# Decoding weights in steps of 1024 columns and starting the gate products a chunk earlier in a three-layer kernel on one core

## The chip, the core and the metric

The kernel runs on one core of a Trainium2 chip. TensorE (PE) does the matrix products, VectorE (DVE), ScalarE (ACT) and GpSimd (POOL) work on tiles in the on-chip memory, SyncE (SP) and GpSimd issue DMA transfers. The metric is the device time of one execution in microseconds (us); smaller is better.

## What is computed

Three layers, one after the other, for 4 x 768 = 3072 tokens. A retention layer (linear attention with a decay per head, 8 heads of 64), then two feed-forward layers:

```
state = gamma * state + k_t v_t^T ;  y_t = scale * q_t state
h = (x @ w1) * (x @ w2) @ w3 ;  x = h @ w_out
h = x @ w_in ;  g = h * sigmoid(1.702 h) ;  out = g @ w_out
```

x is 3072 x 512; w1 and w2 are 512 x 1024, w3 1024 x 1024, the first w_out 1024 x 512, w_in 512 x 2048, the last w_out 2048 x 512. q, k and v are float32. The weights are handed to the core as the 64-bit words of float64 numbers and turned into float32 there.

## The kernel before

**Precision.** Every large product is done three times in the fast float32 format: a matrix is split into a high part and a low part (the residue), and `mm3` multiplies high by high, high by low, low by high.

**Weights.** 36 tiles (`tiles`): 8 of w1 and w2 together (the gate), 4 of w_out, 8 of w3, 16 of the last layer. A tile has two halves. `fetch` loads a raw half, 128 x 512 words of 8 bytes, into one of five buffers; the first two by GpSimd's queue, the others by SP's. Three of the early ones are `held`: VectorE first writes a few zeros into the buffer, so that the load can't be issued before VectorE has come to that place. `magnitude` (ScalarE) takes the absolute value of the high words into `x`. `weight_steps` is a generator whose steps run on VectorE: clamp (line 196), shift (204), or-in of the low words (208), sign (218), all in place in x and by halves of 512 columns. Then `upper` (ScalarE, 145) casts x to the high part `wh` and `lower` (VectorE, 150) subtracts it to get the low part `wl`; both by halves. The low parts of a tile are made after the clamp of the next. That is ten steps a tile (`TILE_OPS`). Tiles of the last layer (`seven`) go through GpSimd into DRAM.

**Order.** The program is written out by hand; each engine runs its instructions in the order in which the program issues them. `work(n)` advances the decode by n steps, so a table of numbers decides where decode stands between other work.

**Attention.** 24 chunks of 128 tokens (c = 0 to 23; six per batch). In the turn of chunk c: vs (v with its decay, ScalarE and GpSimd) and the scores `s` of chunk c+1 (line 376, into one bank that all chunks share), the products `y` with the state (431), the mask of chunk c+1 (`pt`, 394, VectorE), the state's update `u` (407) and copy (419), the products `y` with pt (442), the outputs `xb` (463), the load of a later chunk of qkv (357, GpSimd's queue, 1 MB). Between these stand four places at which `fill(c, at)` adds other work (at = 0 to 3). xb goes to DRAM (`xd`, SP's queue) or, for two blocks of 512 tokens, is split into xh and xl at once.

**Gate within the attention.** From the chunk with c = 9 on, at the end of a turn, half a gate tile of the first token block is multiplied (`first_gate`, lines 259 to 261: for each of four k-blocks wh by xh, wh by xl, wl by xh) into one bank, `wide` (psg). At the start of the next turn `first_out` copies the bank to h (ScalarE, 995) or multiplies h by it (VectorE, 997). Fifteen halves fit before the last chunk ends; the sixteenth follows in a loop behind it.

**Behind the attention.** The other five blocks go through the gate (`gate_mm`, banks psm, eight tiles each) with a number of decode steps per tile, and eight products of w3 and w_out (`mix_mm`, psw) stand among them as soon as their tiles are decoded. From there on the layers are products of blocks in a seven-product scheme: `blend`, `Expand`, `contract`.

The numbers that steer the decode in the attention, four per chunk (one per place), are:

```
PACE = dict.fromkeys(range(5, 9), (0, 2, 0, 0))
PACE.update({9: (0, 2, 0, 5), 10: (0, 1, 0, 5)})
work(PACE.get(c, (0, 1, 0, 4))[at])
```

Of the kernel before, what the change touches and what calls it, by code (L numbers as in the profile page):

```python
# [7 lines left out]
F32 = mybir.dt.float32  # L8
F32R = mybir.dt.float32r
# [25 lines left out]
LEAST, MOST = 2.0, (1 + 0x680000 / 2**23) * 2.0**32  # L35
TILE_OPS = 10
PACE = dict.fromkeys(range(5, 9), (0, 2, 0, 0))
PACE.update({9: (0, 2, 0, 5), 10: (0, 1, 0, 5)})
NM = KF // 2
# [8 lines left out]
def tile_kernel(  # L48
# [49 lines left out]
    WO, W3, WI = 8, 12, 20  # L98
    raws, wx, parts = {}, {}, {}
    homes = {"wg": big}  # L100
# [33 lines left out]
    def magnitude(i):  # L134
        if i >= len(tiles):
            return
        xs = wx.setdefault(i, [])
        for raw in raws.get(i, [])[len(xs) :]:
            x = prep.tile([P, WC], F32, tag="x", bufs=6, name="x")
            high = raw[:, :, 1].bitcast(F32)  # L140
            nc.scalar.activation(x, high, AF.Abs, scale=2.0**16)  # L141
            xs.append(x)

    def upper(i, n):
        nc.scalar.copy(parts[i][0][:, n * WC : (n + 1) * WC], wx[i][n])

    def lower(i, n):
        at = slice(n * WC, (n + 1) * WC)
        hi, lo = (x[:, at] for x in parts[i])
        nc.vector.tensor_tensor(lo, wx[i][n], hi.bitcast(F32), ALU.subtract)  # L150

# [38 lines left out]
    def weight_steps():  # L190

        nonlocal used
        for i in range(len(tiles)):
            magnitude(i)
            for x in wx[i]:
                nc.vector.tensor_scalar(x, x, LEAST, MOST, ALU.max, ALU.min)
                yield i - (len(lows) > 0)
            for k, f in enumerate(lows):
                f()
                yield i - 1 + k  # L200
            lows.clear()
            for x in wx[i]:
                bits = x.bitcast(I32)
                nc.vector.tensor_scalar(bits, bits, 3, None, ALU.logical_shift_left)
                yield i
            for x, raw in zip(wx[i], raws[i]):
                bits = x.bitcast(I32)
                nc.vector.scalar_tensor_tensor(
                    bits, raw[:, :, 0], 29, bits, ALU.logical_shift_right, ALU.bitwise_or
                )  # L210
                yield i
            if i:
                magnitude(i + 1)
            if i < WI:
                parts[i] = wtile(tiles[i][1])
            for n, (x, raw) in enumerate(zip(wx[i], raws[i])):
# [3 lines left out]
                )  # L220
                if i < WI:
                    upper(i, n)
                used += 1
                fetch()
                fetch()
                if i:
                    magnitude(i + 1)
# [3 lines left out]
            if i < WI:  # L231
                lows[:] = [lambda i=i, n=n: lower(i, n) for n in range(2)]
            if i == 0:
                for k, f in enumerate(lows):
                    f()
                    yield k
                lows.clear()

# [3 lines left out]
    ALL = 10**6  # L242
    limit = TILE_OPS * KF + 6

# [42 lines left out]
    def gate_half(t, m, key, ps):  # L287

        w = [x.rearrange("p (m k f) -> p m k f", m=2, k=KD) for x in weight(t)]
        xh, xl = xhl[key]  # L290
        for d in range(KD):
            mm3(ps, w[0][:, m, d], w[1][:, m, d], xh[:, d], xl[:, d], d == 0, d == KD - 1)

# [566 lines left out]
    def opening(t):  # L860
# [11 lines left out]
        if t == 6:  # L872
            hi2["k3"] = prep.tile([P, TB], F32R, tag="x", bufs=6, name="h3")
            split_h(0, 3, 4, hi2["k3"].rearrange("p (a t) -> p a t", a=1))
# [81 lines left out]
    with tc.manual_schedule():  # L956
# [4 lines left out]
        with (  # L961
# [11 lines left out]
            for c in range(2, 6):  # L973
                attention.load(c)
            for _ in range(2):
                fetch(queue=nc.gpsimd)
            attention.factors(1)
# [23 lines left out]
            def fill(c, at):  # L1001
                for _ in range((c, at) in ((6, 0), (7, 0), (8, 0))):
                    fetch(held=True)
                if at == 3 and c > 2 * CPB and halves // 2 < min(complete, KF):
                    first_gate(wide)
                if at == 0:
                    while late:
                        first_out(*late.pop())
                if at == 1 and c in (*range(2, 6), *range(10, 14)):
                    hi, lo, x = first_x.pop(0)  # L1010
                    nc.scalar.copy(hi, x)
                    engine = nc.vector if c > 2 * CPB else nc.gpsimd
                    engine.tensor_tensor(lo, x, hi.bitcast(F32), ALU.subtract)
                if c > CPB:
                    work(PACE.get(c, (0, 1, 0, 4))[at])
                if (c, at) == (8, 2):
                    magnitude(1)

            attention.run(fill)
            free = [wide] + [  # L1020
                y[:, j].rearrange("p n t -> p (n t)") for y in attention.y for j in range(2)
# [8 lines left out]
        with (  # L1030
# [69 lines left out]
            for n, i in list(enumerate(ORDER))[1:]:  # L1100
                nxt = ORDER[n + 1] if n + 1 < NB else None
                for t in range(KF):
# [10 lines left out]
                    if nxt is not None and t in range(KD - 1, KF - 1):  # L1113
                        split_x(nxt, t - KD + 1)
                    work(((8, 6, 3, 3)[n - 1] + (n < 4) * (t % 2)) if n < 5 else (t < 4) + (t < 5))
                    (gate_second if n > 2 else gate_first)(t, i, ab)
                    while rows < KF and (complete > W3 + rows or (n, t) == (2, KF - 1)):
                        ps = mix_mm(rows)
                        work(7)
                        mix_out(rows, ps)  # L1120
# [156 lines left out]
```

## Time and profile before

| | us |
|---|---|
| median of 3 runs | 972.88 (972.52 to 973.39) |
| the profiled execution | 973.11 |
| its span, first to last instruction | 971.3 |
| TensorE busy | 952.3 (98%) |
| weight loads of TensorE, beside its products | 826.0 |
| VectorE busy | 719.3 |
| ScalarE busy | 424.4 |
| GpSimd busy | 229.4 |
| granted TensorE clock, mean | 0.999 |

Busy times are sums over the span, and stages differ. Where a wait is shown, the name behind the arrow is what came last before the instruction could start; "issue" means that nothing shown held it. An "x2" behind a row of the timeline is two instructions, and the time before it is that of both.

### The profile page before, as it was taken

To read this page: it belongs to the slowest core of one execution; us is meant where nothing else is said; L and a number is where in the kernel's file an instruction comes from. 1 tells how busy PE (TensorE), PEld (TensorE's weight loads), DVE (VectorE), ACT (ScalarE), POOL (GpSimd) and SP (SyncE) were. 2 spreads that over 40 slices of the span, in tenths; PEclk is the share of its full clock that TensorE was granted. 3 is DMA by queue.
4 is the path that set the end of the run, shared out by engine and by line. 5 is a ranking of instruction groups with operands and counts; after the bars stand their busy time and mean duration, and the time that the engine had idled before them with its cause. 6 is when DMAs were issued, how large, how long until landed. Compare 5 with 4: busy or idle time off the path is not lost.

```text
span 971.3 us, 15570 instructions
## 1 busy us (share of the span) xinstructions
PE 952.3 (98%) x5992; PEld 826.0 (85%) x5992; DVE 719.3 (74%) x943; ACT 424.4 (44%) x691; POOL 229.4 (24%) x281
## 2 busy tenths in 40 slices
PE   6899999999999999999999999999999999999998
PEld 5678778888888888888889999999998888888886
DVE  6898878889889886766687976948686665566662
ACT  4555444433222222654536654554555544353430
POOL 6422100478787875330020000000000000000000
PEclk9999999999999999999999999999999999999999
DMA  9999766579898999899778546464696968767871
GB/s 349 400 350 350 281 214 202 199 246 359 314 365 288 357 338 395 306 334 312 248 254 305 226 171 246 203 250 184 253 348 252 339 222 271 254 196 230 290 233 50
DMA packets 112618, 266.74 MB, mean 275 GB/s; under 512 B 7872, under 2 KB 67264, under 8 KB 103456
## 3 DMA queue, kind: packets, MB, share of 16 engines
q1 hardware_dynamic: 96560, 186.64, 54.8%
q0 software_dynamic: 15840, 78.91, 21.4%
q8 instruction: 47, 0.77, 0.3%
q14 instruction: 27, 0.22, 0.1%
q10 hardware_dynamic: 144, 0.20, 0.1%
HBM read 164.53 MB, written 101.19 MB: 274 GB/s over the span
## 4 chain that ended last, share of the span: by engine, by line
PE 90%; DVE 4%; DMA 3%; issue 1%; ACT 1%; POOL 0%; DVEq 0%; POOLq 0%; ACTq 0%; SPq 0%
PE m L259 12%; PE m L260 12%; PE m L261 12%; PE psm L261 7%; PE psm L260 7%; PE psm L259 7%; PE a L260 4%; PE a L261 4%; PE a L259 4%; PE e L260 2%; PE e L259 2%; PE e L261 2%; PE psg L259 2%; PE y L442 2%; PE s L376 1%; DMA raw<-in_w_dram 1%
## 5 line engine op out<-in xcount | busy, mean ns | idle before, releaser
L260 PE MATMUL psm<-xl,wh 128*128 128x512 f32 x320 | 124.5, 389 | 0.0
L259 PE MATMUL psm<-xh,wh 128*128 128x512 f32 x320 | 124.5, 389 | 0.0
L261 PE MATMUL psm<-xh,wl 128*128 128x512 f32 x320 | 124.5, 389 | 0.0
L261 PE MATMUL m<-h,op 128*128 128x512 f32 x320 | 124.5, 389 | 0.0
L259 PE MATMUL m<-h,op 128*128 128x512 f32 x320 | 124.5, 389 | 0.0
L260 PE MATMUL m<-l,op 128*128 128x512 f32 x304 | 118.3, 389 | 0.0
L726 ACT CAST h<-l 128x2048 fp32r<-128x2048 f32 x38 | 72.3, 1914 | 85.1 <-PE m L261 56.9
L727 DVE TENSOR_TENSOR l<-l,h 128x2048 fp32r<-128x2048 f32 x38 | 85.7, 2286 | 22.5 <-ACT h L726 22.5
L732 POOL DMA_DIRECT2D op<-sw x6 | 3.2, 532 | 393.0 <-PE a L261 212.7
L260 PE MATMUL a<-yl,op 128*128 128x384 f32 x256 | 85.6, 335 | 0.1
L259 PE MATMUL a<-yh,op 128*128 128x384 f32 x256 | 85.5, 334 | 0.0
L261 PE MATMUL a<-yh,op 128*128 128x384 f32 x256 | 85.5, 334 | 0.0
L141 ACT ACTIVATE x<-raw 128x512 f32<-128x512 f32 x72 | 46.9, 675 | 70.3 <-DMA raw<-in_wo_dram 35.7
L261 PEld LDWEIGHTS m<-h,op 128*128 128x128 f32 x320 | 60.1, 188 | 12.6
L260 PEld LDWEIGHTS psm<-xl,wh 128*128 128x128 f32 x320 | 60.1, 188 | 12.6
L259 PEld LDWEIGHTS psm<-xh,wh 128*128 128x128 f32 x320 | 60.1, 188 | 12.5
L259 PEld LDWEIGHTS m<-h,op 128*128 128x128 f32 x320 | 60.1, 188 | 12.4
L261 PEld LDWEIGHTS psm<-xh,wl 128*128 128x128 f32 x320 | 60.1, 188 | 12.3
L260 PEld LDWEIGHTS m<-l,op 128*128 128x128 f32 x304 | 57.1, 188 | 11.8
L259 PE MATMUL m<-h,wh 128*128 128x512 f32 x168 | 65.4, 389 | 0.0
L261 PE MATMUL m<-h,wl 128*128 128x512 f32 x168 | 65.4, 389 | 0.0
L175 DVE TENSOR_TENSOR l<-l,h 128x2048 fp32r<-128x2048 f32 x19 | 43.6, 2292 | 26.1 <-ACT h L274 24.6
(172 smaller groups left out, 2198.1 us busy)
## 6 DMA issues: line engine op xcount, KB each, us to landing
gd<-g SPq DMA_DIRECT2D x32, 1344.0 KB, 5.0
qkv<-in_qkv_dram POOLq DMA_DIRECT2D x20, 1024.0 KB, 9.2
l<-gd SPq DMA_DIRECT2D x26, 768.0 KB, 7.4
l<-hd SPq DMA_DIRECT2D x19, 1024.0 KB, 7.4
raw<-in_w_dram SPq DMA_DIRECT2D x30, 512.0 KB, 5.9
hd<-g POOLq DMA_DIRECT2D x12, 1280.0 KB, 7.2
raw<-in_wo_dram SPq DMA_DIRECT2D x24, 512.0 KB, 6.8
l<-gd SPq DMA_DIRECT2D x24, 512.0 KB, 5.2
```

The costliest lines, as they stand in the source:

```text
L141: nc.scalar.activation(x, high, AF.Abs, scale=2.0**16)
L175: nc.vector.tensor_tensor(lo, x, hi.bitcast(F32), ALU.subtract)
L259: nc.tensor.matmul(ps, wh, xh, start=start, stop=False, skip_group_check=True)
L260: nc.tensor.matmul(ps, wh, xl, start=False, stop=False, skip_group_check=True)
L261: nc.tensor.matmul(ps, wl, xh, start=False, stop=stop, skip_group_check=True)
L376: nc.tensor.matmul(self.s[u * D : (u + 1) * D, j, p, t], qkt[c][r, 1, p, u * D : (u + 1) * D], qkt[c][r, 0, p, t], start=True, stop=True, ...
L442: nc.tensor.matmul(out_y, vs[c][:, 2 * p + j, :], pt[c][:, j, p, :], start=(c % NCK == 0 and p < 2), stop=True, skip_group_check=True,)
L726: nc.scalar.copy(hi, x.bitcast(F32))
L727: nc.vector.tensor_tensor(x, x.bitcast(F32), hi.bitcast(F32), ALU.subtract)
L732: queue.dma_start(t.bitcast(F32), sw[PART[name]])
```

## The change

**Decode.** The two halves of x are one tile of 1024 columns (`whole`). Clamp, shift, high part and low part are one instruction each; or-in and sign, which read raw words, stay in halves. A tile has seven steps. The numbers of `work` are new accordingly.

**ScalarE's part.** `upper` and the magnitudes of the next tile are put into a list (`later`) while the attention runs, and the list is emptied at place 0 of a chunk's turn behind `first_out` (the gate's copy), or just before `lower` needs it.

**Start.** The decode starts at c = 4 instead of 5, the held loads stand at c = 5, 6, 7 instead of 6, 7, 8, the magnitudes of tile 1 at c = 7 instead of 8, gate halves at c = 8 instead of 9. The first two raw halves are loaded ahead of qkv chunks 4 and 5 on GpSimd's queue instead of behind 5.

**Within a gate half** the eight products with wh come first, then the four with wl.

```
-TILE_OPS = 10
-PACE = dict.fromkeys(range(5, 9), (0, 2, 0, 0))
-PACE.update({9: (0, 2, 0, 5), 10: (0, 1, 0, 5)})
+TILE_OPS = 7
+PACE = {4: (0, 1, 0, 0), 5: (0, 1, 0, 1), 6: (0, 1, 0, 1), 7: (0, 1, 0, 1)}
...
-            x = prep.tile([P, WC], F32, tag="x", bufs=6, name="x")
+            if not xs:
+                whole[i] = prep.tile([P, 2 * WC], F32, tag="x", bufs=3, name="x")
+            x = whole[i][:, len(xs) * WC : (len(xs) + 1) * WC]
...
-    def upper(i, n):
-        nc.scalar.copy(parts[i][0][:, n * WC : (n + 1) * WC], wx[i][n])
+    def upper(i):
+        nc.scalar.copy(parts[i][0], whole[i])
...
+    def lower(i):
+        hi, lo = parts[i]
+        nc.vector.tensor_tensor(lo, whole[i], hi.bitcast(F32), ALU.subtract)
+
+    def flush():
+        while later:
+            later.pop(0)()
+
+    def when_free(f):
+        later.append(f)
+        if not deferred:
+            flush()
...
-            for x in wx[i]:
-                nc.vector.tensor_scalar(x, x, LEAST, MOST, ALU.max, ALU.min)
-                yield i - (len(lows) > 0)
-            for k, f in enumerate(lows):
-                f()
-                yield i - 1 + k
-            lows.clear()
-            for x in wx[i]:
-                bits = x.bitcast(I32)
-                nc.vector.tensor_scalar(bits, bits, 3, None, ALU.logical_shift_left)
+            x = whole[i]
+            bits = x.bitcast(I32)
+            nc.vector.tensor_scalar(x, x, LEAST, MOST, ALU.max, ALU.min)
+            yield i - (len(lows) > 0)
+            if lows:
+                flush()
+                lows.pop()()
                 yield i
+            nc.vector.tensor_scalar(bits, bits, 3, None, ALU.logical_shift_left)
+            if i:
+                when_free(lambda i=i: magnitude(i + 1))
+            yield i
...
-                if i < WI:
-                    upper(i, n)
+                if i < WI and n:
+                    when_free(lambda i=i: upper(i))
...
-        for d in range(KD):
-            mm3(ps, w[0][:, m, d], w[1][:, m, d], xh[:, d], xl[:, d], d == 0, d == KD - 1)
+        h, l = (x[:, m] for x in w)
+        todo = [(h[:, d], x[:, d]) for d in range(KD) for x in (xh, xl)]
+        todo += [(l[:, d], xh[:, d]) for d in range(KD)]
...
-            for _ in range(2):
-                fetch(queue=nc.gpsimd)
+                if c in (3, 4):
+                    fetch(queue=nc.gpsimd)
...
-                for _ in range((c, at) in ((6, 0), (7, 0), (8, 0))):
+                for _ in range((c, at) in ((5, 0), (6, 0), (7, 0))):
                     fetch(held=True)
-                if at == 3 and c > 2 * CPB and halves // 2 < min(complete, KF):
+                if at == 3 and c >= 2 * CPB and halves // 2 < min(complete, KF):
                     first_gate(wide)
                 if at == 0:
                     while late:
                         first_out(*late.pop())
+                    flush()
...
-                if c > CPB:
-                    work(PACE.get(c, (0, 1, 0, 4))[at])
-                if (c, at) == (8, 2):
+                if c >= CPB:
+                    work(PACE.get(c, (0, 1, 0, 2 + c % 2))[at])
+                if (c, at) == (7, 2):
                     magnitude(1)
...
+            deferred = False
+            flush()
...
-                    work(((8, 6, 3, 3)[n - 1] + (n < 4) * (t % 2)) if n < 5 else (t < 4) + (t < 5))
+                    work((6, 4 + t % 2, 2 + t % 2, 2 + (t % 3 == 1), (t < 4) + (t < 5))[n - 1])
...
-                        work(7)
+                        work(5)
```

Three places show what moved. In the order of ScalarE, around the high part of tile 0 (state is the copy of the attention's state, x the magnitudes, wh the high part, vs the values of a chunk), before:

```order
L419 COPY state_130<-u 128x256
L368 ACTIVATE vs<-qkv,dv 128x64 x4
L145 CAST wh<-x 128x512 x2
L419 COPY state_131<-u 128x256
L141 ACTIVATE x<-raw 128x512 x2
```

and after:

```order
L432 COPY state_130<-u 128x256
L143 ACTIVATE x<-raw 128x512 x2
L147 CAST wh<-x 128x1024
L381 ACTIVATE vs<-qkv,dv 128x64 x4
L432 COPY state_131<-u 128x256
```

The cast of tile 0 stood ahead of the magnitudes of tile 1 (the third and fourth raw half) and now stands behind them; it has moved one chunk forward.

On VectorE, the same stretch (L394 and L407 are the masks of the scores, L463 and L476 the outputs), before, from the mask of chunk 6 to one step past that of chunk 8:

```order
L394 TENSOR_TENSOR pt<-s,mask 128x1024
L196 TENSOR_SCALAR x<-x 128x512 x2
L463 TENSOR_TENSOR xb<-y_135,dy 128x512
L130 MEMSET raw 128x2
L394 TENSOR_TENSOR pt<-s,mask 128x1024
L204 TENSOR_SCALAR x<-x 128x512 x2
L463 TENSOR_TENSOR xb<-y_134,dy 128x512
L130 MEMSET raw 128x2
L394 TENSOR_TENSOR pt<-s,mask 128x1024
L208 SCALAR_TENSOR_TENSOR x<-raw,x 128x512 x2
```

and after, over the same masks:

```order
L407 TENSOR_TENSOR pt<-s,mask 128x1024
L213 TENSOR_SCALAR x<-x 128x1024
L476 TENSOR_TENSOR xb<-y_135,dy 128x512
L219 SCALAR_TENSOR_TENSOR x<-raw,x 128x512
L130 MEMSET raw 128x2
L407 TENSOR_TENSOR pt<-s,mask 128x1024
L219 SCALAR_TENSOR_TENSOR x<-raw,x 128x512
L476 TENSOR_TENSOR xb<-y_134,dy 128x512
L227 SCALAR_TENSOR_TENSOR x<-raw,x 128x512
L407 TENSOR_TENSOR pt<-s,mask 128x1024
L227 SCALAR_TENSOR_TENSOR x<-raw,x 128x512
```

Shift, or-in and sign of tile 0 now stand where clamp, shift and the first or-in stood.

On SP's queue, from its first store of outputs on (raw is a raw half, xd a store of outputs), before:

```order
L470 DMA xd_72<-xb 128x512 x2
L131 DMA raw<-in_w_dram 128x1024
L470 DMA xd_72<-xb 128x512
L131 DMA raw<-in_w_dram 128x1024
L470 DMA xd_72<-xb 128x512
L131 DMA raw<-in_w_dram 128x1024 x6
```

and after:

```order
L483 DMA xd_72<-xb 128x512
L131 DMA raw<-in_w_dram 128x1024
L483 DMA xd_72<-xb 128x512
L131 DMA raw<-in_w_dram 128x1024
L483 DMA xd_72<-xb 128x512
L131 DMA raw<-in_w_dram 128x1024 x3
L483 DMA xd_72<-xb 128x512
L131 DMA raw<-in_w_dram 128x1024 x4
```

Each of the first raw halves on this queue has one store less ahead of it; two were loaded by GpSimd, so these are the third, the fourth and so on.

## Rows read from the trace of the kernel before

**Rows 1.** The page, part 1: busy us (share of the span) and instructions.
```profile
PE 952.3 (98%) x5992; PEld 826.0 (85%) x5992; DVE 719.3 (74%) x943; ACT 424.4 (44%) x691; POOL 229.4 (24%) x281
```

**Rows 2.** Stretches: length, busy us of the engines, granted clock, DMA share, GB/s.
```profile
0.00:10.00 10.00, 1.94 (x42) 1.80 (x46) 2.47 (x3) 2.55 (x6) 6.00 (x16) 1.00 0.78 254
10.00:60.00 50.00, 44.49 (x967) 37.14 (x962) 42.32 (x59) 27.48 (x81) 23.39 (x31) 1.00 1.01 401
120.00:180.00 60.00, 59.13 (x284) 47.96 (x283) 48.93 (x91) 25.29 (x44) 5.86 (x7) 1.00 0.60 201
180.00:960.00 780.00, 779.89 (x3756) 685.43 (x3755) 570.13 (x704) 337.77 (x481) 182.93 (x210) 1.00 0.77 273
960.00:971.30 11.30, 6.84 (x31) 5.33 (x29) 1.45 (x3) 0.00 (x0) 0.00 (x0) 0.96 0.14 47
```

**Rows 3.** Waits of TensorE, whole span: us in total, times, longest.
```profile
PE s L376 <- DMA qkv<-in_qkv_dram: 6.0, 4, 4.6
...
PE s L376 <- issue: 1.8, 2, 1.1
...
PE psg L259 <- ACT h L995: 0.7, 1, 0.7
...
PE psw L261 <- DVE wl L150: 0.2, 1, 0.2
```

**Rows 4.** Timeline of TensorE: start, us, line, out<-in, count [idle before].
```profile
36.09 0.39 PE L407 MATMUL u<-vs,qkv 128*64 128x64 f32 x6 [1.47 <-issue]
...
39.07 1.05 PE L442 MATMUL y<-pt,vs 128*64 128x128 f32 x16
...
40.60 0.79 PE L376 MATMUL s<-qkv 64*64 64x128 f32 x25 [0.49 <-DMA qkv<-in_qkv_dram]
...
42.54 0.34 PE L376 MATMUL s<-qkv 64*64 64x64 f32 x4 [1.14 <-issue]
...
44.84 0.50 PE L259 MATMUL psg<-xh,wh 128*128 128x512 f32 x1
...
47.79 0.90 PE L376 MATMUL s<-qkv 64*64 64x128 f32 x32
...
56.13 0.47 PE L259 MATMUL psg<-xh,wh 128*128 128x512 f32 x1 [0.27 <-DVE h L997]
...
125.78 0.50 PE L259 MATMUL psg<-xh,wh 128*128 128x512 f32 x1 [0.68 <-ACT h L995]
```

**Rows 5.** Timeline of ScalarE around the casts of the first gate tiles.
```profile
40.10 1.22 ACT L145 CAST wh<-x 128x512 fp32r<-128x512 f32 x2 [1.51 <-DVE x L218]
...
44.10 0.70 ACT L141 ACTIVATE x<-raw 128x512 f32<-128x512 f32 x1 [1.95 <-DMA raw<-in_w_dram]
...
53.46 0.68 ACT L141 ACTIVATE x<-raw 128x512 f32<-128x512 f32 x1 [1.82 <-DMA raw<-in_w_dram]
```

**Rows 6.** Timeline of SP's queue: a store and the fourth raw half.
```profile
27.56 4.36 SPq L470 DMA_DIRECT2D xd<-xb  x2
...
34.38 0.66 SPq L131 DMA_DIRECT2D raw<-in_w_dram  x1
```

**Rows 7.** DMA issues at 31.97 and 34.38: count, KB, us to landing.
```profile
raw<-in_w_dram SPq DMA_DIRECT2D x1, 512.0 KB, 6.5
...
raw<-in_w_dram SPq DMA_DIRECT2D x1, 512.0 KB, 9.7
```

**Rows 8.** DMA queues, 27.5 to 30.0 and 40.2 to 54: packets, MB, share.
```profile
q0 software_dynamic: 140, 1.01, 98.0%
...
q0 software_dynamic: 479, 3.53, 62.6%
q1 hardware_dynamic: 654, 2.08, 37.4%
```

**Rows 9.** VectorE from 10 to 120 us, by form: count | busy, mean ns | idle before.
```profile
L394 DVE TENSOR_TENSOR pt<-s,mask 128x1024 f32<-128x1024 f32 x23 | 28.1, 1221 | 10.1 <-PE s L376 10.1
L150 DVE TENSOR_TENSOR wl<-x,wh 128x512 fp32r<-128x512 f32 x15 | 10.1, 681 | 0.1
```

More of the change, by code (lines that the diff above doesn't have):

```diff
@@ L98, in tile_kernel @@
     WO, W3, WI = 8, 12, 20
-    raws, wx, parts = {}, {}, {}
+    raws, wx, whole, parts = {}, {}, {}, {}
+    later, deferred = [], True
     homes = {"wg": big}
@@ L142, in magnitude @@
             xs.append(x)
-    def upper(i, n):
-        nc.scalar.copy(parts[i][0][:, n * WC : (n + 1) * WC], wx[i][n])
[L147 to L150, printed above, removed]
+    def upper(i):
[10 more added lines that the diff above has]
+            flush()
     def store_parts(i, a1, a2, st):
@@ L211, in weight_steps @@
                 yield i
-            if i:
-                magnitude(i + 1)
             if i < WI:
@@ L225, in weight_steps @@
                 fetch()
-                if i:
+                if i and not deferred:
                     magnitude(i + 1)
@@ L231, in weight_steps @@
             if i < WI:
-                lows[:] = [lambda i=i, n=n: lower(i, n) for n in range(2)]
+                lows.append(lambda i=i: lower(i))
             if i == 0:
[L234 to L237, printed above, removed]
+                flush()
+                lows.pop()()
+                yield 1
     steps = weight_steps()
@@ L242, in tile_kernel @@
     ALL = 10**6
-    limit = TILE_OPS * KF + 6
+    limit = TILE_OPS * KF + 4
     def work(n):
@@ L290, in gate_half @@
         xh, xl = xhl[key]
-        for d in range(KD):
-            mm3(ps, w[0][:, m, d], w[1][:, m, d], xh[:, d], xl[:, d], d == 0, d == KD - 1)
+        h, l = (x[:, m] for x in w)
+        todo = [(h[:, d], x[:, d]) for d in range(KD) for x in (xh, xl)]
+        todo += [(l[:, d], xh[:, d]) for d in range(KD)]
+        for n, (a, x) in enumerate(todo):
+            nc.tensor.matmul(
+                ps, a, x, start=n == 0, stop=n == 3 * KD - 1, skip_group_check=True
+            )
     def gate_mm(t, key, tile):
@@ L872, in opening @@
         if t == 6:
-            hi2["k3"] = prep.tile([P, TB], F32R, tag="x", bufs=6, name="h3")
+            hi2["k3"] = prep.tile([P, 2 * WC], F32R, tag="x", bufs=3, name="h3")[:, :TB]
             split_h(0, 3, 4, hi2["k3"].rearrange("p (a t) -> p a t", a=1))
@@ L1013, in fill @@
                     engine.tensor_tensor(lo, x, hi.bitcast(F32), ALU.subtract)
-                if c > CPB:
-                    work(PACE.get(c, (0, 1, 0, 4))[at])
-                if (c, at) == (8, 2):
+                if c >= CPB:
+                    work(PACE.get(c, (0, 1, 0, 2 + c % 2))[at])
+                if (c, at) == (7, 2):
                     magnitude(1)
             attention.run(fill)
+            deferred = False
+            flush()
             free = [wide] + [
```

## Prediction

> **What bounds the kernel now.** I read the page's first part, then a table of stretches, then who TensorE waited for, then the timeline of the stretch in which it waits. TensorE is busy 952.3 us of a span of 971.3 [rows 1]. The reader is to see where the other 19.0 us lie [rows 2]: 8.06 in the first 10 us, before inputs and mask have arrived, and 4.46 behind the last products; no line of the diff touches those two. The attention stretch from 10 to 60 us loses 5.51, the stretch from 120 to 180 loses 0.87. These 6.4 us are the most that the change can win (0.65%), unless it makes TensorE's work itself shorter. It does not: the products are the same in number and shape, and only the order within a gate half differs.
>
> In the waits [rows 3] the attention stretch splits into waits for qkv (the 4.6 belongs to the first 10 us, so 1.4 are left) and gaps marked "issue" (1.8 before scores alone, and 1.47 in the update at 36.09 [rows 4]), in which no semaphore held TensorE. All of these lie ahead of the first gate half. The timeline shows the last of them: 1.47 at 36.09, 0.49 before the scores at 40.60, 1.14 in the middle of those scores. From the first gate half at 44.84 on, TensorE runs nearly without a gap; 0.27 at 56.13 and 0.68 at 125.78 remain. VectorE is busy 42.32 of those 50 us and the DMA engines have 1.01 [rows 2], so data and decode are both tight just there.
>
> **The change part by part.**
>
> *The gate one chunk earlier.* A gate half moves from the tenth chunk to the ninth, ahead of the scores at 40.60, and all sixteen halves lie within the chunks. Chunk 8's last products start at 39.07 and take 1.05, so TensorE comes free at 40.12. Where the half can start at once, it covers the 0.49 (qkv arrives meanwhile) and most likely the 1.14 (TensorE goes through 12 products in the 2.9 us instead of some 80); everything behind is a chunk ahead, so the 0.27 goes; and the sixteenth half no longer waits for the copy of its neighbour out of one bank, since two attention product groups stand between (0.68 goes). Sum: 2.58. Every microsecond by which the first half starts after 40.15 takes one back; at 42.73 nothing is left.
>
> *What the first half waits for.* It needs wh of tile 0. Before, ScalarE casts it at 40.10, in two halves of some 0.61, right behind VectorE's sign step, and only then takes the magnitudes of tile 1 [rows 5]. After, the order on ScalarE is the other way round: two magnitudes of tile 1, then one cast of 1024. So wh of tile 0 now stands behind the landing of the fourth raw half. In the trace its magnitude ran at 44.10, after a wait of 1.95 for that DMA [rows 5], which had been issued at 34.38 and took 9.7 [rows 6, 7]. After, it is issued behind only two stores instead of three, one decode step earlier, which I put at 32.6. Its latency is not shown for that place. The nearest rows are 9.7 for the same half and 6.5 for the one before it [rows 7]: it lands between 39.1 and 42.3, and at worst at 44.1 as before, if the earlier place in the queue is worth nothing. Behind it come a magnitude (0.68) and the cast (two halves are 1.22, one should be about 1.15), so the first gate half starts at 41.0, 44.2 or 46.0. I take a landing at 41.3, somewhat nearer to the later row because the same transfers stand around it, and thus a start at 43.1: 43.1 - 40.15 - 2.58 = 0.4 us **lost**. The bounds are 1.7 won and 3.3 lost.
>
> What decides inside this is how SP's queue fares against POOL's. The rows say: badly. From 27.5 to 30.0 POOL's queue has 98.0% of the engines' time [rows 8], though SP issued a store at 27.56 [rows 6]; between 40.2 and 54 SP's queue gets 37.4%, 2.08 MB in 13.8 us [rows 8]. The Trainium skill (DMA: Bandwidth & Descriptors, Queues, rings and completion order) says that each engine goes round robin between the queues for which it has work, a packet at a time. By that rule the raw half would not stand behind POOL's backlog; the result is the second rival below. The first row does not agree with it, the second does roughly.
>
> *VectorE's merged steps.* Per tile two clamps, two shifts and two subtractions become three steps of 1024. A 1024-column tensor step takes 1.221 (from PSUM), two of 512 take 2 x 0.681 = 1.36 [rows 9]; so 0.14 for a subtraction, and I put 0.1 for each of the others: 0.3 to 0.4 per tile, 12 us over 36 tiles. It lies beside TensorE's work; TensorE waits for VectorE only for 0.27 and 0.2 us behind the first ten [rows 3, 4]. On the path: 0. Against it stands that clamp and shift of tile 0 now lie a chunk earlier, ahead of masks that TensorE needs; about 1 us of delay at the mask of chunk 7, which I count at nothing because the first gate half waits for wh anyway (its price is 1.0 if wh is early).
>
> The rule that speaks against the merge is in the Trainium skill (Trace Analysis, Optimizing Scalar/DVE Operations): grouping helps an engine that is saturated, and where an engine merely makes others wait, shorter instructions get work done sooner. The trace bears it out here: of the cast at 40.10 the gate's first half needs only the first 512 columns, so with the split form it could start about 0.55 earlier than I forecast.
>
> *Low weights last; the gate's copy first.* The twelve products of a half take 2.95, from 44.84 to the scores at 47.79 [rows 4]; eight of them, some 1.9, now run before wl is needed, and before, the third product needed it. That pays for wl being one step of 1024 (1.2). Worth 0 either way. The gate's copy ahead of the magnitudes keeps the bank free in time: part of the 0.27 and 0.68 above.
>
> *Paces behind the attention.* Tiles have 7 steps for 10 and the numbers are scaled along; the products of the mixed weights come three, three and two instead of two, three and three at the same places. There wl is late by 0.2 [rows 3]; as one step of 1024 it may be 0.5 later, on one or two rows: 0 to 1 us, and I take 0.1. From 180 to 960 TensorE has no gap worth naming, and VectorE's part gets smaller.
>
> **Sum.** The profiled execution took 973.11. 973.11 + 0.4 + 0.1 = 973.6; the median of the three runs is 972.88, which is 0.23 lower: **973.4**. A measurement of this kernel can tell about 0.2% from no change, 1.95 us: this is no change.
>
> **The rivals.**
>
> *The raw data come in time* (0.22). If SP's transfers get their turn at once, the fourth half lands by 39.1, wh is there at 41.0, and the decode delay of 1.0 is then the only loss: 1.6 won, at best 2.58. 970.3 to 971.3, say 971.2. For it: the raw half before it took 6.5 only. Against it: SP's share in rows 8. (The Trainium skill's rule above is this case.)
>
> *The sixth raw half holds the third gate half* (0.17; the slower side). Before, ScalarE waited for that half until 53.46 [rows 5] and the third gate half began at 56.13, 2.67 later. After, the third half is wanted a chunk earlier: 11.4 us behind the first, at 54.5 in my forecast. Ahead of it stand again a magnitude, a clamp (now ahead of the multiplication that frees the bank), the multiplication, and a low part behind a mask: some 3.3 us. It decides from a landing at 51.2 on; if the half comes no earlier than before, the third gate half begins at 56.7 and 2.2 us are added to my forecast: 975.6. For it: with five raw halves asked for earlier, SP's queue at 0.15 MB/us has the same backlog. Against it: one store less stands ahead.
>
> *Other gaps close too* (0.06). The "issue" gaps of 1.47 and the two smaller ones lie in chunks whose timing shifts. If VectorE's later masks cover them, up to 2.6 more are won: 968.7 to 970.
>
> *The change does nothing that shows* is inside my forecast, since the merged steps are hidden.
>
> **How the numbers follow.** Forecast 0.55, with starts of the first half between 42 and 44, so 972.3 to 974.3. The range leaves out the best of the early cases and the worst of the late: 971.1 to 975.7. Faster than 970.93: 0.06 and a third of the first rival, 0.14. Slower than 974.83: 0.17 and 0.05 from late starts in my own case, 0.22. The rest, 0.64, is no change.
>
> **What would show it.** Right: in the timeline of the new kernel the first gate half stands ahead of the scores of chunk 10, begins around 43 with the wait put down to ScalarE's cast, the cast directly behind a magnitude that waited for a raw DMA; the scores behind it have no gap; the 0.68 is gone; the idle time from 10 to 60 us is 5 to 6 us. Early raws: a start at 41 or before, and 4 us idle. Late raws: a wait of over 1 us at the third gate half. Wrong altogether: idle time behind 180 us, or TensorE busy for another time than 952 us.

## The result and the profile after

The change makes the kernel slower: 982.94 us (median of 6 runs, 980.26 to 984.43) against 972.88, a ratio of 1.0100, 95% interval 1.0085 to 1.0115. The profiled execution took 983.11 with a span of 981.3, 10.0 us more than before. One of the ten executions of mag_late_cast_first, an experiment below, took 1531.21 us at a granted clock of 0.58; it is counted in that run's median (976.55; 976.45 without it) and in no ratio.

The first part of the page of the changed kernel (busy us, share of the span, instructions), to set beside [rows 1]:

```profile
PE 955.5 (97%) x5992; PEld 827.5 (84%) x5992; DVE 708.4 (72%) x850; ACT 421.9 (43%) x671; POOL 231.1 (24%) x281
```

VectorE has 719.3 - 708.4 = 10.9 us less to do, as intended. TensorE has 3.2 us more with the same 5992 products, so some of them ran slower. The table of stretches of the changed kernel (columns as in [rows 2], with the granted clock ahead of the last two):

```profile
10.00:60.00 50.00, 42.91 (x900) 35.55 (x901) 37.89 (x47) 25.07 (x74) 22.96 (x29) 0.97 0.97 381
...
120.00:180.00 60.00, 54.96 (x323) 44.25 (x322) 44.76 (x65) 22.77 (x34) 0.00 (x0) 0.94 0.57 190
180.00:240.00 60.00, 60.00 (x266) 49.67 (x266) 49.03 (x59) 21.90 (x34) 36.13 (x43) 1.00 0.75 248
240.00:960.00 720.00, 719.86 (x3491) 635.60 (x3490) 518.37 (x605) 318.12 (x447) 152.48 (x175) 1.00 0.77 276
```

Against [rows 2], the attention stretch lost 1.6 us of busy time, the stretch from 120 to 180 us lost 4.2, and in both the granted clock fell below 1. Behind 180 us nothing is lost. The longest waits of TensorE for work of other engines in the changed kernel, 10 to 240 us (us in total, times, longest), to set beside [rows 3]:

```profile
PE psw L269 <- DVE wl L151: 2.8, 1, 2.8
PE psg L303 <- ACT wh L147: 2.5, 1, 2.5
PE psw L267 <- ACT wh L147: 2.2, 1, 2.2
```

Three waits that were not there before, all for decoded weights. One (psg) is the first gate half, which the prediction spoke of. The other two (psw) are in the first product of mixed weights behind the attention.

**The attention** ends 2.8 us later: the first product of the gate behind it (psm) begins at 131.40 instead of 128.63. TensorE in the changed kernel around the first gate half (start, us, what, idle before):

```profile
39.80 1.05 PE L455 MATMUL y<-pt,vs 128*64 128x128 f32 x16
43.38 0.50 PE L303 MATMUL psg<-xh,wh 128*128 128x512 f32 x1 [2.54 <-ACT wh L147]
...
45.05 0.63 PE L303 MATMUL psg<-xh,wh 128*128 128x512 f32 x1
45.47 0.63 PE L303 MATMUL psg<-xl,wh 128*128 128x512 f32 x1
45.90 1.91 PE L303 MATMUL psg<-xh,wl 128*128 128x512 f32 x4
47.74 1.02 PE L389 MATMUL s<-qkv 64*64 64x128 f32 x32
```

and ScalarE at the same time:

```profile
41.73 0.66 ACT L143 ACTIVATE x<-raw 128x512 f32<-128x512 f32 x1 [3.52 <-DMA raw<-in_w_dram]
42.30 1.03 ACT L147 CAST wh<-x 128x1024 fp32r<-128x1024 f32 x1
43.23 1.06 ACT L381 ACTIVATE vs<-qkv,dv 128x64 f32<-128x64 f32 x4
```

The cast to wh stands behind a magnitude that waited 3.52 us for its raw half, and the gate half starts when the cast is done. That is the mechanism of the prediction, which had the start at 43.1. What it did not have is the second half of the rows: from 44.6 on a product follows its neighbour in 0.42 us instead of 0.23. The gate half takes 47.74 - 43.38 = 4.36 us instead of 2.95. The attention's account: 0.73 lost ahead of it (the products y start at 39.80 instead of 39.07), 2.54 idle, 1.41 at the lower clock, 0.67 of waiting for a wl at 69.63, less the 2.58 of closed gaps, which are indeed gone: 2.77.

**Behind the attention** 7.2 us are lost (from the first psm to the end of the span: 849.9 against 842.67). TensorE there:

```profile
166.44 0.50 PE L267 MATMUL psw<-wh 128*128 128x512 f32 x1 [2.23 <-ACT wh L147]
...
169.98 0.79 PE L269 MATMUL psw<-wh,wl 128*128 128x512 f32 x1 [2.81 <-DVE wl L151]
170.57 0.63 PE L267 MATMUL psw<-wh 128*128 128x512 f32 x1
```

5.04 us idle, and then nine products in 3.82 us (170.57 to 174.39) that take 2.05 at full clock: 1.8 more. All of it lies at the mixed products: from the first psm to the gate product behind the last psw it is 94.68 us against 87.58 before, 7.1 more, and from there on nothing. Why is the tile late? The wl of tiles 8 and 12 began at 131.38 and 159.97 before, at 134.76 and 168.71 after: the decode lost 5.4 us within four tiles, 2.9 of them in the first. There ScalarE and VectorE do this (the changed kernel):

```profile
134.63 0.67 ACT L143 ACTIVATE x<-raw 128x512 f32<-128x512 f32 x1
140.51 0.66 ACT L143 ACTIVATE x<-raw 128x512 f32<-128x512 f32 x1 [5.21 <-DMA raw<-in_wo_dram]
141.07 0.57 ACT L314 COPY h<-psm 128x512 f32<-128x512 f32 x1
```

```profile
136.62 0.69 DVE L219 SCALAR_TENSOR_TENSOR x<-raw,x 128x512 int32<-128x512 int32 x1
141.68 0.69 DVE L315 TENSOR_TENSOR h<-h,psm 128x512 f32<-128x512 f32 x1 [4.36 <-ACT h L314]
142.28 0.68 DVE L219 SCALAR_TENSOR_TENSOR x<-raw,x 128x512 int32<-128x512 int32 x1
```

and these were ScalarE and VectorE before the change at the same place:

```profile
131.55 0.59 ACT L301 COPY h<-psm 128x512 f32<-128x512 f32 x1
132.04 0.68 ACT L141 ACTIVATE x<-raw 128x512 f32<-128x512 f32 x1
137.77 0.66 ACT L141 ACTIVATE x<-raw 128x512 f32<-128x512 f32 x1 [5.06 <-DMA raw<-in_wo_dram]
```

```profile
134.33 0.69 DVE L302 TENSOR_TENSOR h<-h,psm 128x512 f32<-128x512 f32 x1 [0.99 <-issue]
```

The wait for the raw half is the same, some 5 us. Before, the gate's copy stood ahead of it; after, behind it. VectorE's multiplication by the copy waits 4.36 us instead of 0.99, and the rest of tile 9 (or-in, sign) is queued behind the multiplication. In the code, `when_free` holds back only while the attention runs; behind it, the magnitudes of the next tile are issued at once, right behind the shift, where before they came behind the or-in steps and so behind the copy.

### The profile page after: what moved, and what is told of

Its sections match the earlier page's. It is cut to its first block, busy times and chain, and to the rows that moved or that the text cites. A ratio compares the mean times of both kernels' runs of the same rounds, so it can differ in the third digit from the quotient of the medians.

```text
span 981.3 us, 15406 instructions
## 1 busy us (share of the span) xinstructions
PE 955.5 (97%) x5992; PEld 827.5 (84%) x5992; DVE 708.4 (72%) x850; ACT 421.9 (43%) x671; POOL 231.1 (24%) x281
## 4 chain that ended last, share of the span: by engine, by line
PE 87%; DVE 5%; DMA 4%; issue 2%; ACT 1%; POOL 0%; DVEq 0%; ACTq 0%; SPq 0%; POOLq 0%
PE psm L303 19%; PE m L268 12%; PE m L267 12%; PE m L269 12%; PE psg L303 4%; PE a L268 4%; PE a L269 4%; PE a L267 4%; PE e L268 2%; PE e L267 2%; PE e L269 2%; PE psw L269 2%; PE psw L267 2%; PE psw L268 2%; DMA ck<-in_qkv_dram 1%
## 5 line engine op out<-in xcount | busy, mean ns | idle before, releaser
L303 PE MATMUL psm<-xh,wl 128*128 128x512 f32 x320 | 85.5, 389 | 0.0
L267 PEld LDWEIGHTS m<-h,op 128*128 128x128 f32 x320 | 60.1, 188 | 12.5
L303 PEld LDWEIGHTS psm<-xl,wh 128*128 128x128 f32 x320 | 60.1, 188 | 12.5
L303 PEld LDWEIGHTS psm<-xh,wl 128*128 128x128 f32 x320 | 60.1, 188 | 12.5
```

Source lines behind the costliest of these rows:

```text
L267: nc.tensor.matmul(ps, wh, xh, start=start, stop=False, skip_group_check=True)
L303: nc.tensor.matmul(ps, a, x, start=n == 0, stop=n == 3 * KD - 1, skip_group_check=True)
```

## The experiments

Theory 1: the loss is the order on ScalarE, at two places. Theory 2: the steps of 1024 columns make each tile late. Theory 3: only the place of the mixed products (three, three, two) is wrong. The numbers in the table are medians, and the ratio to the kernel before, run beside them (medians of 973.5 to 973.9 in all four groups). The ratio with its interval goes by all runs of both, so that it can differ from that of the medians by up to 0.001; differences of under 1 us between two versions are not told from none by either.

| run | us | ratio | 95% |
|---|---|---|---|
| mag_late | 977.53 | 1.0043 | 1.0025 to 1.0060 |
| cast_first | 980.95 | 1.0077 | 1.0059 to 1.0095 |
| mag_late_cast_first | 976.55 | 1.0035 | 1.0025 to 1.0046 |
| rows_later | 990.89 | 1.0168 | 1.0144 to 1.0192 |
| split_behind | 981.93 | 1.0077 | 1.0057 to 1.0097 |
| fix_split_behind | 975.68 | 1.0017 | 1.0008 to 1.0027 |
| fix_split_all | 974.09 | 1.0000 | 0.9990 to 1.0011 |
| fix_gate_nine | 979.32 | 1.0059 | 1.0037 to 1.0080 |
| before_mag_early | 981.66 | 1.0087 | 1.0072 to 1.0102 |
| before_lows_last | 974.10 | 1.0003 | 0.9993 to 1.0014 |
| fix_all_rows_later | 974.74 | 1.0007 | 0.9999 to 1.0016 |
| fix_all_state_first | 973.81 | 1.0007 | 0.9994 to 1.0019 |

### The magnitudes behind the copy again (mag_late)

```
-            if i:
+            if i and deferred:
                 when_free(lambda i=i: magnitude(i + 1))
...
+            if i and not deferred:
+                magnitude(i + 1)
             if i < WI:
                 parts[i] = wtile(tiles[i][1])
```

> Behind the attention alone, the magnitudes of the next tile go back to where they stood before, behind the or-in steps, and so behind the gate's copy on ScalarE; all else as in the changed kernel (982.9 us). There the copy of the gate stood behind a magnitude that waited 5.21 us for its raw half, and VectorE's multiplication by it waited 4.36 us. Theory 1 (queue order): the decode of tile 9 gains about 3 us and all later tiles with it; the 5.04 us that TensorE waits at the first product of mixed weights fall to about 2, the time to 977.5 to 980. Theory 2 (the steps of 1024 columns are what makes a tile late, 0.5 us of waiting in each): no gain, 982 to 983. Theory 3 (the product simply stands one gate tile too early): no gain either, 982 to 983.

977.53: 5.4 us of the 10 come back from one swap, by the medians. ScalarE, then TensorE, of the profiled execution (978.97):

```profile
134.10 0.58 ACT L316 COPY h<-psm 128x512 f32<-128x512 f32 x1
...
140.80 0.66 ACT L143 ACTIVATE x<-raw 128x512 f32<-128x512 f32 x1 [5.55 <-DMA raw<-in_wo_dram]
```

```profile
165.79 0.50 PE L271 MATMUL psw<-wh,wl 128*128 128x512 f32 x1 [1.67 <-DVE wl L151]
```

The raw half is no earlier (5.55 us of waiting), but the gate's copy no longer stands behind it. The 5.04 us at the mixed products fall to 2.7 in four smaller waits, the longest 1.67, and the clock there stays at 1.00. From the first psm to the gate product behind the last psw it is 90.97 us: of the 7.1 us that the changed kernel lost there, the order made 3.7, and 3.4 are left with the order right. Theory 1 holds for the larger half; theories 2 and 3 expected nothing from this swap, but what is left is open to them.

### The cast ahead of the magnitudes (cast_first) and both (mag_late_cast_first)

```
                 if (c, at) == (7, 2):
+                    flush()
                     magnitude(1)
```

> In the attention alone: the cast to wh of tile 0 is put ahead of the magnitudes of tile 1 on ScalarE, and so no longer behind the wait for the fourth raw half (3.52 us). Theory 1 (the wait and the clock that falls behind it are the attention's loss): the first gate half starts at about 41 us instead of 43.4, the 2.54 us wait is under 0.5, the granted clock of 45 to 48 us is back from 0.50 to near 1, TensorE reaches the first product of mixed weights 2.5 to 3 us earlier, and the time is about 980. Rival (what stands behind it is late anyway, since the decode behind the attention is bound by its transfers): the wait at that product grows by as much, 982 to 983.

980.95, 2.0 us less; the intervals overlap a little, but the trace shows where it comes from. The first gate half starts without a wait, the granted clock from 44 to 48 us is 1.00 instead of 0.58, and the first psm begins at 129.01, 2.4 us earlier. Gate halves still wait for wl:

```profile
55.71 1.20 PE L303 MATMUL psg<-xh,wl 128*128 128x512 f32 x4 [1.12 <-DVE wl L151]
67.21 1.19 PE L303 MATMUL psg<-xh,wl 128*128 128x512 f32 x4 [0.67 <-DVE wl L151]
```

> Both edits, of the attention and of the magnitudes behind it. If the two losses are separate, the gains add: 974.5 to 977.5. If the decode behind the attention is late by itself, the gain of the attention reappears as a wait at the first products of mixed weights: 978 to 980.

976.55: inside the range for separate losses, and 6.4 of the 10 us are back (the two gains add up to 7.4). The attention ends level with before (psm at 128.82 against 128.63); 1.9 us of waits for wl are left at the mixed products.

### Whole tiles or halves (split_behind, fix_split_behind, fix_split_all)

```
-    def upper(i):
-        nc.scalar.copy(parts[i][0], whole[i])
+    def upper(i, n):
+        at = slice(n * WC, (n + 1) * WC)
+        nc.scalar.copy(parts[i][0][:, at], whole[i][:, at])
...
-        nc.vector.tensor_tensor(lo, whole[i], hi.bitcast(F32), ALU.subtract)
+        for at in (slice(0, WC), slice(WC, 2 * WC)):
+            nc.vector.tensor_tensor(
+                lo[:, at], whole[i][:, at], hi[:, at].bitcast(F32), ALU.subtract
+            )
...
-                if i < WI and n:
-                    when_free(lambda i=i: upper(i))
+                if i < WI:
+                    when_free(lambda i=i, n=n: upper(i, n))
```

This is fix_split_all, on top of both edits. In the other two the halves are used only behind the attention; split_behind has them alone, fix_split_behind with both edits.

> The changed kernel, with wh and wl made by halves of 512 columns again behind the attention alone; the magnitudes stay ahead of the gate's copy there, and the attention is as it was changed (982.9 us). Theory 1 (queue order is the larger part): the 5.21 us wait of the magnitude of tile 9 and VectorE's 4.36 us behind it stay; the halves win back the 0.5 us that wl waits for the whole cast in most tiles and let the first products of mixed weights start on half a tile, 1.5 to 3 us in all: 980 to 981.5. Theory 2 (steps of a whole tile are the larger part): 977 to 979.

981.93, 1.0 us less than the changed kernel, whose own runs spread over 4: no more than a hint, and not theory 2's 4 to 6 us. One of the two waits at the mixed products shrinks to 0.40, the other stays at 2.89.

> Both edits that won time (the cast of tile 0 ahead of the magnitudes in the attention, the magnitudes behind the gate's copy after it: 976.55 us), and wh and wl by halves behind the attention. There the products of mixed weights still waited 1.9 us for wl in three places, 1.0 the longest. If whole-tile steps are what is left: 974 to 975. If not, 976 to 977.

975.68: 0.9 us less, between the two expectations, and too little for the intervals to tell by itself. The wait at the first mixed product is gone; one of 0.89 on a later one is the longest left.

> As the one before, and wh and wl by halves in the attention too. There two gate halves waited 1.49 and 0.67 us for a wl of 1024 columns (1.2 us), of which the first of them needs the first 512 columns alone. If those waits are the merged steps' price: 1 to 2 us less than by halves behind the attention alone, 972.5 to 973.5, level with the kernel before. If they are the price of the earlier start: no less, 974 to 975.

974.09, level with the kernel before. The waits of this version, 5 to 240 us, those for weights:

```profile
PE psw L275 <- DVE wl L153: 1.4, 2, 0.8
...
PE psg L309 <- DVE wl L153: 0.6, 1, 0.6
```

Another 1.6 us came back, as the first expectation has it: with the order right, whole-tile casts and subtractions cost 2.5 us in all (976.55 to 974.09; these intervals are apart). How that splits between the attention and what is behind it, the traces don't show: in them the part from the first psm on shrinks by 1.5 us over the two steps (845.58, 844.67, 844.12), while the first psm stays at 128.8 to 129.2. In the attention the waits for wl did fall from 2.16 to 0.59, but TensorE waited 1.01 us for the copy of the state instead of 0.40.

### What the earlier start is worth (fix_gate_nine)

```
-                if at == 3 and c >= 2 * CPB and halves // 2 < min(complete, KF):
+                if at == 3 and c > 2 * CPB and halves // 2 < min(complete, KF):
```

> Both edits that won time (976.55 us), but gate halves from the chunk with c = 9 on, as before the change: what the earlier start is worth. By the prediction's bounds the start half a chunk earlier is worth 0 to 2.6 us. With the attention of both kernels ending level (the products behind it began at 128.8 us with both edits, at 128.6 before the change), I expect about nothing: 976 to 977.5. If the start is worth what the closed gaps say, 978 to 979.

979.32, 2.8 us more than with both edits alone. I expected nothing, and was wrong. TensorE of this run:

```profile
41.62 0.79 PE L391 MATMUL s<-qkv 64*64 64x128 f32 x25 [1.05 <-DMA qkv<-in_qkv_dram]
...
50.19 0.67 PE L446 MATMUL y<-qkv,state 64*64 64x128 f32 x16 [1.20 <-ACT state L434]
...
58.42 0.50 PE L305 MATMUL psg<-xh,wh 128*128 128x512 f32 x1 [0.83 <-DVE h L1012]
...
128.10 0.50 PE L305 MATMUL psg<-xh,wh 128*128 128x512 f32 x1 [0.67 <-ACT h L1010]
```

The gaps that the earlier start had closed are back: 1.05 and 0.32 at the scores, 0.83 and 0.67 at the bank, 2.87 together, where the prediction had 2.58. That the total moved by nearly the same is in part luck: the wait for the copy of the state grew from 0.40 to 1.20 (on ScalarE it stands behind a magnitude again), the products ahead of the gate half came 0.58 later, and against that the two waits for wl in the attention (1.49 and 0.67) went away. So the level attention of mag_late_cast_first was a gain of 2.6 to 2.9 and a loss about as large: 2.16 of waiting for wl and 0.40 for the state.

### The order alone, put into the kernel before (before_mag_early)

```
-            for x in wx[i]:
+            for n, x in enumerate(wx[i]):
                 bits = x.bitcast(I32)
                 nc.vector.tensor_scalar(bits, bits, 3, None, ALU.logical_shift_left)
+                if behind and n:
+                    magnitude(i + 1)
                 yield i
...
             attention.run(fill)
+            behind = True
```

> The kernel before, with one thing of the change done alone, and behind the attention alone: the magnitudes of the next tile are issued right behind the last shift and so ahead of the gate's copy on ScalarE. Steps, halves, paces and the places of the products are those of before. Theory 1 (queue order): the copy at 131.55 us comes behind the magnitude that ended its wait for a raw half at 137.8, VectorE's multiplication at 134.3 moves to about 139, the decode of tile 9 by 3 to 4 us, and the products of mixed weights, which waited 0.2 us for wl, wait about 3; with the lower clock that stood behind such waits in the changed kernel 976 to 979. Rival (it does harm only with whole-tile steps or the other places of the products): 973 to 974.5.

981.66: of all that the change does, this one order, in otherwise untouched code with halves, ten steps and the old places, costs 8.2 us by the medians, more than I expected. ScalarE, and TensorE, of this run:

```profile
137.43 0.66 ACT L141 ACTIVATE x<-raw 128x512 f32<-128x512 f32 x1 [5.76 <-DMA raw<-in_wo_dram]
137.99 0.57 ACT L304 COPY h<-psm 128x512 f32<-128x512 f32 x1
...
296.40 0.66 ACT L141 ACTIVATE x<-raw 128x512 f32<-128x512 f32 x1 [9.01 <-DMA raw<-in_wo_dram]
296.96 0.57 ACT L304 COPY g<-psm 128x512 f32<-128x512 f32 x1
```

```profile
163.93 0.79 PE L264 MATMUL psw<-wh,wl 128*128 128x512 f32 x1 [2.40 <-DVE wl L150]
297.59 0.50 PE L262 MATMUL psm<-xh,wh 128*128 128x512 f32 x1 [1.69 <-ACT g L304]
```

The expected wait is there (2.40, with a clock of 0.59 from 164 to 168 us): from the first psm to the gate product behind the last psw it is 91.30 us instead of 87.58. These 3.7 us are what mag_late won at the same place. The other 4.0 us lie further on, where the changed kernel loses nothing: the same order does it again at 297 us, where a magnitude waited 9 us with a copy behind it (waits of 1.69, 0.83 and 0.52 us follow, the last two for xl). So the order alone accounts for 3.7 of the 7.1 us behind the attention, shown from both sides; that 8.2 is close to the whole loss is chance. The remaining 3.4 us belong to theories 2 and 3, as far as traces of single executions tell: at the mixed products 2.7 are left in mag_late_cast_first, 1.8 with halves behind the attention, 1.4 with halves everywhere, and nothing with the later place, changed next. How much of the 3.4 each of the two costs by itself is not shown.

### The place of the mixed products (rows_later, fix_all_rows_later)

```
-                    while rows < KF and (complete > W3 + rows or (n, t) == (2, KF - 1)):
+                    while rows < KF and (complete > W3 + rows + 1 or (n, t) == (2, KF - 1)):
```

> Only the place of the products of mixed weights is changed: each needs one tile more decoded ahead of it in the program, so that the first stands one gate tile later. Theory 3 (the place alone is wrong, as the step of the prediction on the paces behind the attention has it): the 5.04 us wait and the lower clock behind it (0.50 in 168 to 172 us, 0.71 in 172 to 176) go, and the time is 975.5 to 977. Rival (the decode is late as a whole, and each product waits where it stands): under half of that comes back, 979 to 982.

990.89, which neither theory had. The 5.04 us are indeed gone (0.53 left), but TensorE waits anew, and the products behind that wait ran at the lower clock, 2.9 us more; this is TensorE and then ScalarE of this run:

```profile
259.67 0.80 PE L303 MATMUL psm<-xh,wh 128*128 128x512 f32 x1 [5.53 <-ACT h L314]
```

```profile
257.94 1.21 ACT L143 ACTIVATE x<-raw 128x512 f32<-128x512 f32 x2 [12.52 <-DMA sp<-x]
259.05 0.57 ACT L314 COPY h<-psm 128x512 f32<-128x512 f32 x1
```

Again the gate's copy behind magnitudes, which this time waited 12.5 us for a free x (the stores of finished tiles to DRAM hold it). A later place puts these steps beside other gate tiles, and the same order bites there.

> The version with both edits and halves everywhere (974.1 us), and each product of mixed weights one tile of decode later in the program. Done alone, this took the 5.04 us wait away but gave a new one of 5.5 us at 260 us, where the gate's copy stood behind a magnitude that had waited 12.5 us for a free x. If that one is the same queue order, it is gone here with the magnitudes behind the copy: the 1.4 us that wl still costs at these products go too, 972.5 to 973.5. If the later place itself costs (the decode then has too little time up to the last layer), 975 or more.

974.74, and 0.6 more than fix_split_all, which the intervals don't separate. With the copy ahead, the new wait is gone, and so are those for wl: behind the attention TensorE has no wait left but one of 0.2 us, and the time from the first psm to the end is that of before (842.8 against 842.67). The later place costs nothing once the order is right. Its profiled run was late in the attention instead (the first psm at 130.67).

### The state's copy ahead of tile 2's magnitudes (fix_all_state_first)

```
-            if i and deferred:
+            if i > 1 and deferred:
...
+                if (c, at) == (9, 2):
+                    magnitude(2)
```

ScalarE in fix_all_rows_later:

```profile
49.26 0.68 ACT L143 ACTIVATE x<-raw 128x512 f32<-128x512 f32 x1 [3.54 <-DMA raw<-in_w_dram]
51.55 0.66 ACT L143 ACTIVATE x<-raw 128x512 f32<-128x512 f32 x1 [1.61 <-DMA raw<-in_w_dram]
52.11 0.35 ACT L438 COPY state<-u 128x256 f32<-128x256 f32 x1
```

> The version with both edits, halves everywhere and the products of mixed weights a tile later (974.7 us), and one swap on ScalarE in the attention: the copy of the state stands ahead of the two magnitudes of tile 2, which there waited 3.54 and 1.61 us for raw halves and held the copy back (TensorE's products with the state waited 2.19 us for it). Behind the attention that version had no wait left. If this hold is what is left of the loss: 1 to 2 us less, 972.5 to 973.7, level with the kernel before or just below it. If the next thing behind it (vs of the next chunk, still behind the same magnitudes) is as late: 974 to 975.

973.81 against 973.83 for the kernel before. The wait for the state is gone (2.19 before the swap), the first psm begins at 128.62. By the medians the gain is 0.9, of the size expected; by the ratios (1.0007 with and without the swap) there is none. In its place stands a wait of 1.38 for a wl at 55.92. No version here beats the kernel before.

### Low weights last (before_lows_last)

```
-        for d in range(KD):
-            mm3(ps, w[0][:, m, d], w[1][:, m, d], xh[:, d], xl[:, d], d == 0, d == KD - 1)
+        todo = [(h[:, d], x[:, d]) for d in range(KD) for x in (xh, xl)]
+        todo += [(l[:, d], xh[:, d]) for d in range(KD)]
```

> The kernel before, with one other thing of the change done alone: within a gate half the eight products with wh come first, then the four with wl. By the prediction this costs and wins nothing: 973 to 974 (before: 973.5 to 973.9 in the last runs). If a gate half waited for wl unseen, up to 0.7 us less.

974.10, ratio 1.0003: nothing that shows, as predicted.

## Why the prediction was wrong

**First gate half: right.** The fourth raw half was issued at 32.67 (I put 32.6), took 9.0 us (between the 6.5 and 9.7 of [rows 7]), and the half started at 43.38 (43.1). The Trainium skill (DMA: Bandwidth & Descriptors, Queues, rings and completion order) has the queues served in turn, which was my first rival. The 9.0 us don't decide about that rule: while the half was under way, from 32.67 to 41.7, SP's queue had 62.7% of the engines' time and moved 2.20 MB, so the half shared its own queue with other transfers. What did not come is the rival's landing by 39.1. The closed gaps were right too: 2.58 by the rows, and 2.87 in the trace of fix_gate_nine. The idle time from 10 to 60 us was 7.1 us and not 5 to 6.

**No term for the clock: wrong by some 3 us.** The sum priced a wait at its length. The 2.54 us wait was followed by 1.4 us of slower products, the 5.04 us by 1.8 more. In the attention this is most of what lies between the 0.4 us of the sum and the measured 2.8.

**Merged steps, "on the path: 0": wrong by 2.5 us where the order is right** (976.55 with whole tiles, 974.09 with halves); in the changed kernel itself the price is not shown clear of noise (1.0 in split_behind, and 0.67 of waiting at 69.63). They were to be hidden since TensorE had hardly waited for VectorE before. But the change itself brought the first consumer closer: at 55.7 and 67 us once the first gate half starts in time (cast_first), and at the mixed products. The Trainium skill's rule (Trace Analysis, Optimizing Scalar/DVE Operations), weighed there against the merge, is what these runs agree with: the version with the shorter casts and subtractions was faster by 2.5 us.

**"Paces behind the attention", 0 to 1 us, taken as 0.1: the step that failed.** It measured 7.2: 5.04 of waiting, 1.8 at the lower clock, and 0.4, nearly all of it the first product behind the second wait, whose neighbour follows in 0.59 us instead of 0.23. By cause, 3.7 are the order on ScalarE, and 3.4 are left with the order right, for whole tiles and the place together. I looked at wl's duration there and at which product comes in which place, and carried over "the gate's copy first" from the attention, the only stretch where `later` holds anything back. Behind it the order turned round: magnitudes ahead of the copy. The trace of before had the price in it, a magnitude that waited 5.06 us at 137.77 with the copy ahead of it; I had priced the same mechanism at the first gate half and did not look for it at the second place. Correcting that one order won 5.4 us and making it alone in the kernel before lost 8.2 by the medians; at the mixed products both were 3.7.

**The rivals.** The early raw halves did not come. The sixth raw half was waited for (magnitude at 50.10 after 1.03 of waiting), but landed ahead of the 51.2 from which my rival decides; what it held was not the gate half but the copy of the state, for which TensorE did not wait here. "Wrong altogether" named idle time behind 180 us, where there is none: the loss stood at 166, inside a stretch that I had counted as full. It also named TensorE busy for another time than 952 us, and that came: 955.5, by the lower clock.

## What to carry to other kernels

An instruction that waits for a transfer also holds everything issued behind it on its engine, so when a change moves such an instruction, list for each stage of the program what now stands behind it and who waits for that; a harmless wait of 5 us in the old trace is the price of the new order. When steps are merged because an engine is busy, look first at who needs the first half of the result. Where one edit wins and three lose, take them apart: here the earlier start was worth 2.6 to 2.9 us, and its companions took it all back and 10 more. And see where in the trace a loss lies before two totals are set equal: 8.2 us of one order was 3.7 at the place in question.

## What the runs showed of the hardware

The granted clock fell to 0.50 (1.2 of 2.4 GHz) behind some waits and not behind others. The stretches of the changed kernel around the two waits (columns as above):

```profile
44.00:48.00 4.00, 4.00 (x17) 2.73 (x19) 3.97 (x6) 1.67 (x8) 0.00 (x0) 0.58 1.01 421
...
164.00:168.00 4.00, 0.94 (x3) 0.30 (x2) 2.41 (x5) 2.62 (x4) 0.00 (x0) 0.94 0.48 145
168.00:172.00 4.00, 2.02 (x5) 1.63 (x6) 3.97 (x7) 1.16 (x2) 0.00 (x0) 0.50 0.33 130
172.00:176.00 4.00, 4.00 (x15) 3.16 (x14) 3.48 (x6) 1.62 (x2) 0.00 (x0) 0.71 0.58 174
```

It also fell behind the 2.21 us at the first gate half of mag_late, the 2.40 us of before_mag_early, the 2.19 us of fix_all_rows_later (0.60 from 52 to 54 us) and the 5.53 us of rows_later, and stayed at 1.00 behind the 1.67 us of mag_late and the 1.69 us of before_mag_early. It did not fall at once everywhere: behind the 2.54 us of the changed kernel the first products still followed each other in 0.23 us, up to 44.6. Where it fell, it added 1.4 and 1.8 us to the waits of the changed kernel and 2.9 us to that of rows_later. What decides, beside the length of the wait, is open.

At the start of the span the column is no guide to how fast the products run. It reads 1.00 from 8 to 20 us in the changed kernel, with a wait of 3.50 us that ends in it, but the 32 products of a chunk's scores took 1.56 us behind that wait and 0.90 a chunk later:

```profile
9.81 1.56 PE L389 MATMUL s<-qkv 64*64 64x128 f32 x32 [3.50 <-DMA qkv<-in_qkv_dram]
...
14.23 0.90 PE L389 MATMUL s<-qkv 64*64 64x128 f32 x32
```
